# Attention and MLP on one core: the last 64 keys in one load per tensor, q and k turned by one 1024-column DMA transpose

## The chip, the core and the metric

The kernel runs on one NeuronCore of a Trainium2 chip. The metric is the device time of one execution in microseconds (us). Three executions of the kernel before took 483.74 to 487.81 us, with a median of 485.37.

## The reference

The program computes softmax attention and feeds its output to a two-layer MLP:

```python
# q, k, v: (8, 12, 448, 64)
scores = scale * np.matmul(q, k.transpose(0, 1, 3, 2))
attn = softmax(scores)                                  # over the keys
attn_out = np.matmul(attn, v)
x = attn_out.transpose(0, 2, 1, 3).reshape(B * S, H * D)  # (3584, 768)
h = x @ w_in                                            # w_in (768, 2048)
out = np.maximum(0.01 * h, h) @ w_out                   # w_out (2048, 768)
```

All inputs and the output are float32; inside, the kernel works in bf16 with float32 sums.

## The kernel before, in words

The attention is cut into 48 units, each of one batch and two heads (`NU = B * HP`, u = 6 b + hp). A sequence of 448 rows is 4 times 112 for the queries (`SC`, `NSC`) and 3 times 128 plus 64 for the keys (`NKC`, `KR`).

`load(u)` brings q, k and v of a unit from memory: q in one DMA (L108), the first 384 keys of k and of v of both heads in one DMA each (L115), and the last 64 keys, called the tail here, in one DMA per head and tensor (L120), head 0 to partitions 0 to 63 and head 1 to partitions 64 to 127. That makes seven loads. Except for unit 0 all are issued by SyncE, whose DMA queue is called SP here. `cast(u)` turns them to bf16 on POOL (L130, L131, L137 for q and k, L138 and L144 for v) and lays q and k of both heads side by side in one tile qkb: 4 x 128 columns of q in 112 partitions, then 3 x 128 columns of k, then 128 columns in which the tails of the two heads stand block by block (head 0 in partitions 0 to 63 and columns 0 to 63, head 1 in the others, zeros elsewhere).

qkb is then transposed, so that the head dimension lies on the partitions. For the first 12 units (`NPE`) TensorE does it (L207, L209) and VectorE copies the result to qkT (L212). From unit 12 on `dma_transposes` does it by two DMA transposes on SP (L194, from `turn`), the q half of 112 rows and the k half of 128 rows, 512 columns each. `scores` multiplies keys and queries (L227 for the 384 keys, L223 for the tails of both heads at once), `expo` takes the exponential on ScalarE, `pv` multiplies by v and normalises. The attention output x of a unit is transposed to xT, from unit 9 on by a DMA transpose on SP too. `mlp(i)` is a generator that works through 384 or 512 rows: 16 steps of w_in (L304), then the steps of w_out (L322), whose results `store` sends out through SP (L286), as a rule in two DMAs.

The order of each engine's work is the order in which the code issues it. The first six units run through `first`. After them the main loop mixes the MLP steps with half units: `event(g)` does in its first half the scores, the cast of unit u+3 and the load of unit u+5, and in its second half the last scores, the second half of pv of the unit before, its xT transpose, and the qkT transposes of unit u+2. `catch_up` calls the events by the share of the MLP's matmul work that is done. mlp(i+1) starts only when the events of its batches are through, and its first matmuls read the xT of the last of these units.

SP is one queue in order: loads, both kinds of transposes and stores pass through it one after the other. An instruction that waits holds all that stand behind it. The DMAs of SP and ScalarE share eight completion semaphores in turn, so each waits for the landing of the DMA eight places before it.

Of the kernel before, what the change touches and what calls it, by code (L numbers as in the profile page):

```python
# [9 lines left out]
F32 = mybir.dt.float32  # L10
# [6 lines left out]
def kernel(  # L17
# [9 lines left out]
    nc = tc.nc  # L27

    B, H, S, D = q.shape
    DM, DF = moe_w_in.shape  # L30
    P = 128
    HP = H // 2
    SC = 112
    NSC = S // SC
# [3 lines left out]
    NKC = 3  # L38
    KR = S - NKC * P
# [9 lines left out]
    ld_pool = ctx.enter_context(tc.tile_pool(name="ld", bufs=5))  # L49
# [30 lines left out]
    NC = 4  # L80
    QC = NSC * P
    qk_sb = [cast_pool.tile([P, QC + (NKC + 1) * P], BF16, name=f"qkb{i}") for i in range(NC)]

    NQ = 4
    QL = S + (NKC + 1) * P
    qkT = [qk_pool.tile([P, QL], BF16, name=f"qkT{i}") for i in range(NQ)]


# [13 lines left out]
    def load(u, queues=(nc.sync,) * 3):  # L102
        if u >= NU:
            return
        b, hp = divmod(u, HP)
        heads = slice(2 * hp, 2 * hp + 2)
        fq = ld_pool.tile([SC, 2, NSC, D], F32, name="fq")
        queues[0].dma_start(  # L108
            out=fq.rearrange("p h so d -> p h (so d)"),
            in_=q[b, heads].rearrange("h (p so) d -> p h (so d)", so=NSC),  # L110
        )
        raw[u] = [fq]
        for a, name, eng in ((k, "fk", queues[1]), (v, "fv", queues[2])):
            t = ld_pool.tile([P, (2 * NKC + 1) * D], F32, name=name)
            eng.dma_start(  # L115
                out=t[:, :2 * NKC * D].rearrange("p (h e) -> p h e", h=2),
                in_=a[b, heads, :NKC * P].rearrange("h (p c) d -> p h (c d)", c=NKC),
            )
            for h in range(2):
                eng.dma_start(  # L120
                    out=t[h * KR:(h + 1) * KR, 2 * NKC * D:], in_=a[b, 2 * hp + h, NKC * P:]
                )
            raw[u].append(t)

    def cast(u, by=(nc.gpsimd.tensor_copy,) * 2):
        if u >= NU:
            return
        fq, fk, fv = raw.pop(u)
        t, vt = qk_sb[u % NC], v_sb[u % NV]
        by[0](t[:SC, :QC].rearrange("p (so h d) -> p h so d", so=NSC, h=2), fq)  # L130
        by[1](  # L131
            t[:, QC:QC + NKC * P].rearrange("p (c h d) -> p h c d", c=NKC, h=2),
            fk[:, :2 * NKC * D].rearrange("p (h c d) -> p h c d", h=2, c=NKC),
        )
        for h in range(2):
            at, c0 = slice(h * KR, (h + 1) * KR), QC + NKC * P + h * D
            by[1](t[at, c0:c0 + D], fk[at, 2 * NKC * D:])  # L137
        nc.gpsimd.tensor_copy(  # L138
            v_whole[u % NV][:, :, :, :D],
            fv[:, :2 * NKC * D].rearrange("p (h c d) -> p h c d", h=2, c=NKC),  # L140
        )
        for h in range(2):
            at, c0 = slice(h * KR, (h + 1) * KR), VL + h * DV
            nc.gpsimd.tensor_copy(vt[at, c0:c0 + D], fv[at, 2 * NKC * D:])  # L144

    w_steps = []
    for i in range(4):
# [1 line left out]
    for i in range(4):  # L149
        at = (slice(None), ts(i % 2, MD // 2), ts(i // 2, NW))  # L150
        w_steps.append((w_out_sb[at], w_out_v[at]))

    def load_w(n=1):
        for _ in range(n):
            if w_steps:
                o, i = w_steps.pop(0)
                nc.gpsimd.dma_start(out=o, in_=i)

    load(0, (nc.sync, nc.scalar, nc.sync))
    for i in range(1, 5):  # L160
        load(i)
# [10 lines left out]
    ident = const_pool.tile([P, P], BF16)  # L172
    make_identity(nc, ident)
    for t in qk_sb:
        nc.gpsimd.memset(t[:, QC + NKC * P:], 0.0)
    for t, tw in zip(v_sb, v_whole):
        nc.gpsimd.memset(tw[:, :, :, D:], 1.0)
        nc.gpsimd.memset(t[:, VL:], 0.0)
        for h in range(2):
            nc.gpsimd.memset(t[h * KR:(h + 1) * KR, VL + h * DV + D:VL + (h + 1) * DV], 1.0)  # L180
    for t in e_sb:
        nc.gpsimd.memset(t[:, EL:], 0.0)
    cast(0, (nc.vector.tensor_copy, nc.scalar.copy))
    load_w()
    cast(1)
    cast(2)


# [4 lines left out]
    def turn(dst, src, rows):  # L193
        nc.sync.dma_start_transpose(out=dst.rearrange("p (c s) -> p c s", s=rows), in_=src)  # L194

    def dma_transposes(u):
        if NPE <= u < NU:
            turn(qkT[u % NQ][:, :S], qk_sb[u % NC][:SC, :QC], SC)
            turn(qkT[u % NQ][:, S:], qk_sb[u % NC][:, QC:], P)

    def transposes(u):
        if u >= min(NPE, NU):
            return
        tr = ps_g.tile([P, QL], BF16, name="tr", tag="g")
        t = qk_sb[u % NC]
        for so in range(NSC):
            nc.tensor.transpose(tr[:, ts(so, SC)], t[:SC, ts(so, P)], ident[:SC, :SC])  # L207
        for c in range(NKC + 1):
            nc.tensor.transpose(  # L209
                tr[:, S + c * P:S + (c + 1) * P], t[:, QC + c * P:QC + (c + 1) * P], ident  # L210
            )
        nc.vector.tensor_copy(qkT[u % NQ], tr)  # L212

    sc_t = {}
# [1 line left out]
    def scores(u, c):  # L216

        ps = ps_s.tile([P, 2, 512], F32, name="sc")
        t = qkT[u % NQ]
        sc_t[u, c] = ps  # L220
        keys = slice(S + c * P, S + (c + 1) * P)
        if c == NKC:
            nc.tensor.matmul(ps[:, 0, :S], t[:, keys], t[:, :S], start=True, stop=True)  # L223
            return
        for j in range(2):
            at = slice(j * D, (j + 1) * D)
            nc.tensor.matmul(ps[:, j, :S], t[at, keys], t[at, :S], start=True, stop=True)  # L227

    def expo(u, c):
        ps = sc_t.pop((u, c))  # L230
# [101 lines left out]
    def first(u):  # L332

        scores(u, 0)
        scores(u, 1)
        expo(u, 0)
        if u == 0:
            warm_up(4)
        expo(u, 1)
        if u >= 2:  # L340
            x_transposes(u - 2)
        if u >= 1:
            pv(u - 1, 0)
        load(u + 5)
        load_w({2: 1, 3: 2, 4: 2, 5: 2}.get(u, 0))
        scores(u, 2)
        expo(u, 2)
        if u + 1 < HP:
            transposes(u + 1)
        scores(u, 3)  # L350
        expo(u, 3)
        cast(u + 3)
        if u >= 1:
            pv(u - 1, 1)


    def event(g):
        u, r = divmod(g, 2)
        back = HP < u <= NU
        if r == 0:  # L360
            if HP < u - 1 < NPE - 3 + 1:
                x_transposes(u - 2)
            if back:
                pv(u - 1, 0)
            if u < NU:
                for c in range(NKC):
                    scores(u, c)
                expo(u, 0)
                expo(u, 1)
                late.append((u, 2))  # L370
            cast(u + 3)
            load(u + 5)
        else:
            if u < NU:
                scores(u, NKC)
                expo(u, NKC)
            if back:
                pv(u - 1, 1)
                if u - 1 >= NPE - 3:
                    x_transposes(u - 1)  # L380
            transposes(u + 1)
            dma_transposes(u + 2)

    transposes(0)
    warm_up(2)
    for u in range(HP):
        first(u)
    u = HP - 1
# [57 lines left out]
```

## Time and profile before

| what | us |
|---|---|
| median of 3 executions | 485.37 |
| lowest, highest | 483.74, 487.81 |
| the profiled execution | 488.74 |
| its span, first to last instruction | 486.9 |
| TensorE matmuls busy (PE) | 426.0 |
| ScalarE busy (ACT) | 213.9 |
| GpSimd busy (POOL) | 124.7 |
| VectorE busy (DVE) | 100.0 |

PE, ACT, POOL and DVE are the four compute engines. Instructions that issue a DMA are not counted as busy on SP; they are read from SP's timeline, where their duration is the time that the queue is held. Granted clock (PEclk) is the share of TensorE's full clock that it was given in a stretch. Times in the rows count from the span's start.

### The profile page before, as it was taken

The numbers are of one execution on the slowest core, as the hardware profiler recorded it, in microseconds if no ns is written. First come the engines' busy times: TensorE is split into PE (matmuls) and PEld (weight loads), VectorE is DVE, ScalarE is ACT, GpSimd is POOL, SyncE is SP. The second block draws the span as 40 slices with busy tenths as digits, with TensorE's granted clock in tenths as the row PEclk, the third lists the DMA queues.
The fourth block names the chain that finished last, engine by engine and source line by source line (L and its number), as shares of the span: only waits on it lengthen the run. The fifth ranks groups of instructions, "written<-read, shape, count | busy, mean of one in ns | idle before, by whom it ended". The sixth has DMA issues, their size and how long they took to land.

```text
span 486.9 us, 9127 instructions
## 1 busy us (share of the span) xinstructions
PE 426.0 (87%) x3491; PEld 245.1 (50%) x3491; DVE 100.0 (21%) x271; ACT 213.9 (44%) x324; POOL 124.7 (26%) x373
## 2 busy tenths in 40 slices
PE   7669989367999999965999989785999989999996
PEld 3445656232556565542556656452456645664463
DVE  2342233110113311220112211221012211130021
ACT  5463644032662366323663257432563445623400
POOL 6446435322213222311311232231132110000000
PEclk9797999787999999997999999998899989999999
DMA  7689997465546655456455664565645662221022
GB/s 156 174 192 192 227 228 186 124 179 132 109 116 153 163 140 131 115 148 174 117 107 123 173 156 104 136 146 142 155 109 129 133 158 59 39 81 43 0 64 67
DMA packets 120396, 64.27 MB, mean 132 GB/s; under 512 B 74272, under 2 KB 116768, under 8 KB 120352
## 3 DMA queue, kind: packets, MB, share of 16 engines
q1 hardware_dynamic: 112624, 57.17, 47.7%
q0 software_dynamic: 7296, 6.29, 8.3%
q8 instruction: 27, 0.44, 0.4%
q10 hardware_dynamic: 432, 0.23, 0.2%
q14 instruction: 17, 0.14, 0.1%
HBM read 45.61 MB, written 11.01 MB: 116 GB/s over the span
## 4 chain that ended last, share of the span: by engine, by line
PE 57%; DMA 20%; SPq 14%; issue 3%; POOL 2%; ACT 2%; DVE 1%; ACTq 0%; POOLq 0%
PE mm L304 26%; PE mm L322 21%; DMA fk<-in_k_dram 8%; SPq L120 6%; DMA fv<-in_v_dram 4%; PE pv L253 4%; PE sc L227 3%; SPq L194 3%; DMA xT<-x 3%; SPq L115 3%; DMA qkT<-qkb 3%; DMA fq<-in_q_dram 2%; SPq L286 2%; ACT e L236 1%; PE pv L246 1%
## 5 line engine op out<-in xcount | busy, mean ns | idle before, releaser
L236 ACT ACTIVATE e<-sc 128x896 bf16<-128x896 f32 x192 | 150.2, 826 | 147.7 <-PE sc L227 117.5
L304 PE MATMUL mm<-xT,w_in_sb 128*128 128x384 bf16 (+1 forms) x768 | 163.8, 369 | 20.6 <-DMA xT<-x 19.6
L322 PE MATMUL mm<-w_out_sb,h 128*128 128x384 bf16 x896 | 154.8, 329 | 0.5 <-DVE x L261 0.2
L304 PEld LDWEIGHTS <-w_in_sb 128*128 128x128 bf16 x768 | 75.1, 101 | 100.1 <-issue 41.6
L322 PEld LDWEIGHTS <-h 128*128 128x128 bf16 x896 | 86.4, 98 | 63.6 <-issue 10.4
L308 ACT ACTIVATE h<-mm 128x384 bf16<-128x384 f32 (+1 forms) x128 | 70.0, 547 | 96.6 <-PE mm L304 96.4
L138 POOL CAST v<-fv 128x384 bf16<-128x384 f32 x48 | 24.3, 506 | 163.0 <-issue 85.8
L326 DVE COPY o<-mm 128x384 f32<-128x384 f32 x56 | 31.2, 557 | 168.9 <-PE mm L322 156.2
L253 PE MATMUL pv<-v,e 128*128 128x65 bf16 x1152 | 59.2, 196 | 0.0
L253 PEld LDWEIGHTS <-e 128*128 128x128 bf16 x1152 | 52.5, 99 | 11.3 <-issue 4.5
L227 PE MATMUL sc<-qkT 64*128 64x448 bf16 x288 | 38.1, 365 | 21.1 <-DMA qkT<-qkb 19.8
L260 DVE RECIPROCAL rec<-pv 112x4 f32<-112x4 f32 x96 | 17.5, 182 | 180.9 <-PE pv L253 177.8
L130 POOL CAST qkb<-fq 112x512 bf16<-112x512 f32 x47 | 28.8, 612 | 91.0 <-DMA fq<-in_q_dram 81.6
L246 PE MATMUL pv<-v,e 128*128 128x130 bf16 x192 | 42.9, 223 | 4.9 <-POOL v L144 3.0
L261 DVE TENSOR_TENSOR x<-pv,rec 112x256 bf16<-112x256 f32 x96 | 40.7, 424 | 3.3
L227 PEld LDWEIGHTS <-qkT 64*128 64x128 bf16 x288 | 10.3, 96 | 30.5 <-DMA qkT<-qkb 21.0
L131 POOL CAST qkb<-fk 128x384 bf16<-128x384 f32 x47 | 23.8, 506 | 5.0 <-DMA fk<-in_k_dram 4.0
L144 POOL CAST v<-fv 64x64 bf16<-64x64 f32 x96 | 22.4, 233 | 8.9 <-DMA fv<-in_v_dram 6.2
L137 POOL CAST qkb<-fk 64x64 bf16<-64x64 f32 x94 | 21.8, 232 | 8.2 <-DMA fk<-in_k_dram 5.2
L246 PEld LDWEIGHTS <-e 128*128 128x128 bf16 x192 | 19.1, 100 | 9.2 <-ACT e L236 1.7
L223 PE MATMUL sc<-qkT 128*128 128x448 bf16 x48 | 17.9, 372 | 0.0
L212 DVE COPY qkT<-tr 128x960 bf16<-128x960 bf16 x12 | 7.9, 657 | 20.3 <-PE tr L209 20.3
(28 smaller groups left out, 54.6 us busy)
## 6 DMA issues: line engine op xcount, KB each, us to landing
fq<-in_q_dram SPq DMA_DIRECT2D x48, 224.0 KB, 3.4
fv<-in_v_dram SPq DMA_DIRECT2D x48, 192.0 KB, 2.7
fk<-in_k_dram SPq DMA_DIRECT2D x47, 192.0 KB, 3.0
w_in_sb<-in_moe_w_in_dram POOLq DMA_DIRECT2D x4, 768.0 KB, 9.6
w_out_sb<-in_moe_w_out_dram POOLq DMA_DIRECT2D x4, 768.0 KB, 23.5
out_dram<-o SPq DMA_DIRECT2D x8, 336.0 KB, 3.0
out_dram<-o SPq DMA_DIRECT2D x8, 288.0 KB, 2.9
out_dram<-o SPq DMA_DIRECT2D x8, 240.0 KB, 3.0
```

The source lines that it names most:

```text
L120: eng.dma_start(out=t[h * KR:(h + 1) * KR, 2 * NKC * D:], in_=a[b, 2 * hp + h, NKC * P:])
L130: by[0](t[:SC, :QC].rearrange("p (so h d) -> p h so d", so=NSC, h=2), fq)
L138: nc.gpsimd.tensor_copy(v_whole[u % NV][:, :, :, :D], fv[:, :2 * NKC * D].rearrange("p (h c d) -> p h c d", h=2, c=NKC),)
L227: nc.tensor.matmul(ps[:, j, :S], t[at, keys], t[at, :S], start=True, stop=True)
L236: nc.scalar.activation(o, i, AX.Exp, scale=scale)
L246: nc.tensor.matmul(ps[:, i].rearrange("p j d -> p (j d)"), e[:, at:at + P], vt[:, VL:], start=True, stop=False,)
L253: nc.tensor.matmul(ps[:, i, j, :], e[:, at:at + P], v_whole[u % NV][:, j, c, :], start=False, stop=(j == 1 and c == NKC - 1),)
L261: nc.vector.tensor_mul(x_t[u][:, ts(half, two)], ps[:SC, :, :, :D], rec.to_broadcast([SC, two, 2, D]))
L304: nc.tensor.matmul(ps[:, :n], w_in_sb[:, kk, ts(m, P)], xT[:, kk, at:at + n], start=(kk == 0), stop=(kk == KD - 1),)
L308: nc.scalar.activation(h[:, m, :n], ps[:, :n], AX.Prelu, alpha=0.01)
L322: nc.tensor.matmul(ps[:, :NW], h[:, m, ts(c, P)], w_out_sb[:, m, ts(w, NW)], start=(m == 0), stop=(m == MD - 1),)
L326: nc.vector.tensor_copy(o[c][:, ts(w, NW)], ps[:, :NW])
```

## The change

The two tail loads of a tensor become one, which puts both heads into partitions 0 to 63, side by side; the casts move the second head to partitions 64 to 127. The q half of qkb and qkT is widened from 4 x 112 to 4 x 128 columns, with zeros in partitions 112 to 127 of qkb's q half (a new memset per tile), so that q and k are one block of 1024 columns; one DMA transpose, or eight equal ones on TensorE, turns it. The scores read 112 of every 128 query columns.

```diff
-    QL = S + (NKC + 1) * P
+    QL = QC + (NKC + 1) * P
...
-            t = ld_pool.tile([P, (2 * NKC + 1) * D], F32, name=name)
+            t = ld_pool.tile([P, 2 * (NKC + 1) * D], F32, name=name)
...
-            for h in range(2):
-                eng.dma_start(
-                    out=t[h * KR:(h + 1) * KR, 2 * NKC * D:], in_=a[b, 2 * hp + h, NKC * P:]
-                )
+            eng.dma_start(
+                out=t[:KR, 2 * NKC * D:].rearrange("m (h d) -> m h d", h=2),
+                in_=a[b, heads, NKC * P:].rearrange("h m d -> m h d"),
+            )
...
-            by[1](t[at, c0:c0 + D], fk[at, 2 * NKC * D:])
+            by[1](t[at, c0:c0 + D], fk[:KR, (2 * NKC + h) * D:(2 * NKC + h + 1) * D])
...
-            nc.gpsimd.tensor_copy(vt[at, c0:c0 + D], fv[at, 2 * NKC * D:])
+            nc.gpsimd.tensor_copy(
+                vt[at, c0:c0 + D], fv[:KR, (2 * NKC + h) * D:(2 * NKC + h + 1) * D]
+            )
...
+        nc.gpsimd.memset(t[96:, :QC], 0.0)
...
-            turn(qkT[u % NQ][:, :S], qk_sb[u % NC][:SC, :QC], SC)
-            turn(qkT[u % NQ][:, S:], qk_sb[u % NC][:, QC:], P)
+            turn(qkT[u % NQ], qk_sb[u % NC], P)
...
-        for so in range(NSC):
-            nc.tensor.transpose(tr[:, ts(so, SC)], t[:SC, ts(so, P)], ident[:SC, :SC])
-        for c in range(NKC + 1):
-            nc.tensor.transpose(
-                tr[:, S + c * P:S + (c + 1) * P], t[:, QC + c * P:QC + (c + 1) * P], ident
-            )
+        for c in range(QL // P):
+            nc.tensor.transpose(tr[:, ts(c, P)], t[:, ts(c, P)], ident)
...
-        keys = slice(S + c * P, S + (c + 1) * P)
+        keys = slice(QC + c * P, QC + (c + 1) * P)
+        qT = t[:, :QC].rearrange("p (so s) -> p so s", s=P)[:, :, :SC]
+        o = ps[:, :, :S].rearrange("p j (so s) -> p j so s", s=SC)
...
-            nc.tensor.matmul(ps[:, j, :S], t[at, keys], t[at, :S], start=True, stop=True)
+            nc.tensor.matmul(o[:, j], t[at, keys], qT[at], start=True, stop=True)
```

How this moves SP's queue is shown at two places. The first is one round of the main loop near 220 us, between the store that goes out there and the next one; fq, fk and fv are the loaded tiles, out_dram is the result. Before:

```order
L286 DMA out_dram<-o 96x768
L286 DMA out_dram<-o 32x768
L108 DMA fq<-in_q_dram 112x2x256
L115 DMA fk<-in_k_dram 128x2x192
L120 DMA fk<-in_k_dram 64x64 x2
L115 DMA fv<-in_v_dram 128x2x192
L120 DMA fv<-in_v_dram 64x64 x2
L194 DMA_TRANSPOSE xT<-x 128x4x112
L194 DMA_TRANSPOSE qkT_113<-qkb_109 128x4x112
L194 DMA_TRANSPOSE qkT_113<-qkb_109 128x4x128
```

The same round with the change (lines are those of the changed kernel):

```order
L286 DMA out_dram<-o 96x768
L286 DMA out_dram<-o 32x768
L108 DMA fq<-in_q_dram 112x2x256
L115 DMA fk<-in_k_dram 128x2x192
L119 DMA fk<-in_k_dram 64x2x64
L115 DMA fv<-in_v_dram 128x2x192
L119 DMA fv<-in_v_dram 64x2x64
L197 DMA_TRANSPOSE xT<-x 128x4x112
L197 DMA_TRANSPOSE qkT_113<-qkb_109 128x8x128
```

The order is the same; of the twelve DMAs of the round nine are left.

The second place is the start of SP's queue, up to the first load of unit 2, the third load of q. Before:

```order
L108 DMA fq<-in_q_dram 112x2x256
L115 DMA fv<-in_v_dram 128x2x192
L120 DMA fv<-in_v_dram 64x64 x2
L108 DMA fq<-in_q_dram 112x2x256
L115 DMA fk<-in_k_dram 128x2x192
L120 DMA fk<-in_k_dram 64x64 x2
L115 DMA fv<-in_v_dram 128x2x192
L120 DMA fv<-in_v_dram 64x64 x2
L108 DMA fq<-in_q_dram 112x2x256
```

With the change:

```order
L108 DMA fq<-in_q_dram 112x2x256
L115 DMA fv<-in_v_dram 128x2x192
L119 DMA fv<-in_v_dram 64x2x64
L108 DMA fq<-in_q_dram 112x2x256
L115 DMA fk<-in_k_dram 128x2x192
L119 DMA fk<-in_k_dram 64x2x64
L115 DMA fv<-in_v_dram 128x2x192
L119 DMA fv<-in_v_dram 64x2x64
L108 DMA fq<-in_q_dram 112x2x256
```

The load of q for unit 2 was the twelfth DMA of SP and is now its ninth. (In unit 0 the loads of k are issued by ScalarE, with one instead of two for its tails.)

## Rows read from the trace of the kernel before

**Rows 1.** Waits of TensorE in seven stretches; us in total, times, longest.

```profile
PE sc L227 <- DMA qkT<-qkb: 7.6, 1, 7.6
...
PE mm L304 <- DMA xT<-x: 5.6, 1, 5.6
PE sc L227 <- DMA qkT<-qkb: 1.6, 1, 1.6
...
PE mm L304 <- DMA xT<-x: 5.7, 2, 5.0
PE sc L227 <- DMA qkT<-qkb: 5.3, 4, 2.1
...
PE mm L304 <- DMA xT<-x: 1.6, 1, 1.6
...
PE sc L227 <- DMA qkT<-qkb: 5.3, 4, 2.2
PE mm L304 <- DMA xT<-x: 4.4, 1, 4.4
...
PE mm L304 <- DMA xT<-x: 2.3, 1, 2.3
```

**Rows 2.** Windows (PEclk behind the engines), then TensorE's timeline: start, us, instructions, idle before.

```profile
96.00:108.00 12.00, 9.33 (x62) 4.46 (x63) 1.77 (x5) 4.80 (x6) 2.39 (x7) 0.76 0.65 173
120.00:150.00 30.00, 30.00 (x227) 16.07 (x226) 5.08 (x15) 16.54 (x25) 8.72 (x26) 1.00 0.50 113
...
82.19 2.77 PE L322 MATMUL mm<-w_out_sb,h 128*128 128x384 bf16 x16
97.69 4.81 PE L322 MATMUL mm<-w_out_sb,h 128*128 128x384 bf16 x16
225.63 5.71 PE L304 MATMUL mm<-xT,w_in_sb 128*128 128x512 bf16 x13 [5.01 <-DMA xT<-x]
...
119.64 3.95 PE mm L304 x18
```

**Rows 3.** SP's timeline in one unit from 188 us, and the xT at 223.

```profile
188.22 2.50 SPq L194 DMA_TRANSPOSE qkT<-qkb  x2
190.76 0.57 SPq L108 DMA_DIRECT2D fq<-in_q_dram  x1
191.39 0.45 SPq L115 DMA_DIRECT2D fk<-in_k_dram  x1
191.89 1.12 SPq L120 DMA_DIRECT2D fk<-in_k_dram  x2
193.05 0.59 SPq L115 DMA_DIRECT2D fv<-in_v_dram  x1
193.69 1.11 SPq L120 DMA_DIRECT2D fv<-in_v_dram  x2
...
223.23 1.22 SPq L194 DMA_TRANSPOSE xT<-x  x1
```

**Rows 4.** The DMA transposes by line: ns min/median/max; then us from issue to landing.

```profile
L194 SPq DMA_TRANSPOSE qkT<-qkb x72: 1183/1216/2448, 92.7 to 420.6; - x72
...
DMA to landing us min/median/max: 2.3/2.4/4.4
```

**Rows 5.** Timeline of TensorE at 16.8 and 30.1 us; groups by line (busy, mean ns).

```profile
16.83 0.56 PE L207 MATMUL tr<-ident,qkb 112*128 112x112 bf16 x4 [5.06 <-POOL qkb L130]
...
30.09 0.35 PE L253 MATMUL pv<-v,e 128*128 128x65 bf16 x6
...
L178 POOL MEMSET v<- 128x130 bf16 x5 | 1.1, 213 | 0.0
L137 POOL CAST qkb<-fk 64x64 bf16<-64x64 f32 x94 | 21.8, 232 | 8.2 <-DMA fk<-in_k_dram 5.2
```

**Rows 6.** SP's timeline at the two ends of the backlog from 77 to 113 us.

```profile
76.87 1.43 SPq L108 DMA_DIRECT2D fq<-in_q_dram  x1
...
110.57 1.22 SPq L194 DMA_TRANSPOSE xT<-x  x1
```

More of the change, by code (lines that the diff above doesn't have):

```diff
@@ L220, in scores @@
         sc_t[u, c] = ps
-        keys = slice(S + c * P, S + (c + 1) * P)
+        keys = slice(QC + c * P, QC + (c + 1) * P)
+        qT = t[:, :QC].rearrange("p (so s) -> p so s", s=P)[:, :, :SC]
+        o = ps[:, :, :S].rearrange("p j (so s) -> p j so s", s=SC)
         if c == NKC:
-            nc.tensor.matmul(ps[:, 0, :S], t[:, keys], t[:, :S], start=True, stop=True)
+            nc.tensor.matmul(o[:, 0], t[:, keys], qT, start=True, stop=True)
             return
```

## The prediction

> **What bounds the kernel now.** I read the waits of TensorE first, stretch by stretch, because its busy share says nothing about where it is late. Up to 84 us its waits are few; after that nearly all the idle time has one of two releasers: a DMA transpose of q and k (qkT) or a DMA transpose of an attention output (xT) [rows 1]. Added up from 84 us on: 7.6 + 5.6 + 1.6 + 5.7 + 5.3 + 1.6 + 5.3 + 4.4 + 2.3 = 39.4 us of a span of 486.9. The reader is to see that no row of this group names an arithmetic engine.
>
> The second view is TensorE's timeline around the long waits. The window from 96 us, after the 7.6 us wait, shows a mean granted clock of 0.76, where the window from 120 us, with no wait in it, shows 1.00 (the full 2.4 GHz level). Sixteen output matmuls that take 2.77 us before take 4.81 behind that wait: 2.0 lost. Thirteen matmuls of 512 columns behind the xT wait at 225.63 take 5.71, while 18 take 3.95 in the steady stretch, so 13 should take 2.85: 2.85 lost [rows 2]. The same 5.7 us piece stands behind the xT waits at 113 and 338.
>
> The third view is the DMA queue of SyncE (SP), which issues both transposes. From 188.22 to the xT at 223.23 it issues without a pause worth naming: two halves of qkT 2.50, q 0.57, k 0.45, the two k tails 1.12, v 0.59, two v tails of the same price, then the next xT [rows 3]. x was ready long before the xT of 223.23 was issued; the transpose stood behind the queue. So the waits of 180 to 226 us, and by the same pattern of 84 to 113 and 293 to 339, are a backlog of SP's issue time, not of bytes. Where TensorE is continuously busy (120 to 150) SP has slack and nothing is to be won.
>
> **The change part by part.** *The tails.* Per unit (one batch and two heads) four 16 KB loads become two of 32 KB. A pair costs SP 1.12 us [rows 3]. The merged load has three dimensions, as the k load beside it, which issues in 0.45 with four times as many rows; so I price it as one of the pair, 0.56. With the gap of about 0.04 that goes too, a unit saves 2 x 0.60 = 1.2 us of SP. Ends: nothing saved if it costs the pair's 1.12; 1.4 if it costs the 0.45 of k.
>
> *The transposes.* One instruction of 1024 columns replaces two of 512. The group of 72 has a minimum of 1183 ns and a median of 1216, though half of them read 112 rows and half 128: rows do not set the price [rows 4]. Whether columns do, no row shows, as all have 512. Low end: one price for any width, 1.22, saves 1.27 with its gap. High end: twice, 2.44, saves nothing. I split the 1.22: a plain load's 0.57 [rows 3] as the fixed part, the other 0.65 growing with the columns; then 0.57 + 2 x 0.65 = 1.87, saving 0.63 per unit. The DMA lands 2.4 us after its issue begins [rows 4]; the wide one should land 1.2 us after its issue ends, so no later than the second half does today.
>
> By the Trainium skill, "DMA: Bandwidth & Descriptors", section "Why a DMA increments its semaphore by 16 and not by 1" (the comparison with earlier generations), the sequencer of the generations before pushes one command per tile for a transpose inside SBUF, 262,144 cycles for 8,192 tiles. That speaks against this half of the change: by it the price goes with the tiles and 2.44 is nearer than 1.22. The equal price of 112 and 128 rows neither shows nor excludes it. What it gives is the second case below.
>
> *What SP's saving is worth, stretch by stretch,* each unit in a backlog saving 1.2 + 0.63 = 1.83:
> - 77 to 113 us: from the q load at 76.87 to the xT at 110.57 [rows 6] SP issues five loads and two qkT: 5 x 1.2 + 2 x 0.63 = 7.3. Before 77 the queue is held by landings, as eight DMAs are in flight at most (each waits for the eighth before it); eight now cover 1.6 units instead of 1.1. At the start TensorE idles 5.06 us for the cast of unit 2 [rows 5]; unit 2's first load is the twelfth DMA of SP now and the ninth then, and the last wait for a landing ahead of it is for an earlier one. I put 2.5 on both together (0 to 5). Sum 9.8, below the 14.8 of waits and 2.0 of clock there, so it counts in full.
> - 188 to 226 us: four loads and four qkT, 7.3 of the 10.3 of waits; about half of the clock's 2.85, since a wait of some 3 us is left. Sum 8.8.
> - 263 to 284: two units, more than the wait of 1.6. Sum 1.6.
> - 293 to 339: five of each, 9.15 of 9.7; what is left is too short to cost the clock, 2.85 more. Sum 12.0.
> - 386 to 397: one unit, 1.8 of 2.3. And about 0.7 of the 5.7 of 170 to 230 lies at 170, in front of the backlog; it goes too.
>
> Total 9.8 + 8.8 + 1.6 + 12.0 + 1.8 + 0.7 = 34.7.
>
> *What it adds.* Four memsets of 32x512 on POOL ahead of the first casts: from 213 ns for 130 columns, at most 840 each, likelier 0.5: 2 us of POOL in the first 6 us. The first weight load and the cast of unit 1 move by that much; behind them stand the later casts. The first lands beside earlier loads, and I have charged it inside the 2.5 above. Half of the tail casts now read partitions 0 to 63 and write 64 to 127; no row shows a shifted cast. Nothing to 232 ns more each [rows 5], POOL is idle most of the time, I take nothing. The evacuation of the first 12 units grows from 960 to 1024 columns, under 0.1 us each, beside TensorE's matmuls of the unit before; without that cover it is 1 us in all. The one transpose waits for the k tail's cast where its q half had only the cast of q to wait for; in the stretches of backlog both casts are done units earlier, so nothing; elsewhere what stands behind it on SP is the next unit's loads, which are needed two units later. The scores read q with a step (112 of each 128 columns). Ends: nothing, or each of the four pieces at the price of a matmul of its own, as six of 65 columns take 0.35 us [rows 5], 58 ns each; I take nothing, because a piece inside an instruction has no issue of its own.
>
> What is late next: in 188 to 226, TensorE itself with short rests of xT; at 113, still xT, by some 5 us.
>
> Against the profiled execution, 488.7 with what lies around its span: 488.7 - 34.7 = 454.0. That execution lies 3.4 above the median of 485.4, and some of its surplus is in these waits; I forecast 453.
>
> **The rivals.**
> 1. *The wide transpose costs 2.44* (the page's rule worked out from rows). Only the tails save: 8.5 + 4 x 1.2 + 1.6 + 5 x 1.2 + 1.2 + 0.7 = 22.8, no clock back; 466. For it: nothing in the rows excludes a price by columns. Against it: a plain load shows that a good part of an issue is fixed.
> 2. *It costs 1.22.* 11.0 + 12.7 + 1.6 + 12.6 + 2.3 + 0.7 = 41; 448. For it: rows did not matter.
> 3. *The change doesn't do what it says:* the merged tail costs the pair's 1.12 and the transpose 2.44. SP issues as long as before; within 1%, 485. Against it: k and its tail differ fourfold in rows at about one price.
> 4. *Stepped reading of q slows the scores.* 336 matmuls at half the upper end of about 0.1 us: some 17 us lost where TensorE is the bound; 470.
> 5. *Slower: the wide transpose costs more than the sum of two.* If its price grew as the square of the width, 4.9 us, each unit would cost SP 4.9 - 2.5 - 1.2 = 1.2 more; over the 17 units of the five stretches that is 20 us: 509. It decides from a price of 2.5 + 1.2 = 3.7 us on. For it: the width is unseen in the trace. Against it: 112 and 128 rows are priced alike, which no growing cost suggests.
>
> **How the numbers follow.** Chances: forecast 0.50, rival 1 0.20, rival 2 0.15, rival 3 0.05, rival 4 0.05, rival 5 0.05. The range runs from 441 (rival 2 with the start worth 5 and the median's 3.4 less) to 471 (rivals 1 and 4); outside lie rivals 3 and 5 and the edges. About 1% is what a measurement of this kernel can tell from no change. Faster: the forecast and rivals 1, 2 and 4, 0.90; same 0.05; slower 0.05.
>
> **What would show it.** 96 merged tails on SP near 0.56 us; 36 qkT transposes near 1.9 (1.2 or 2.4 for rivals 2 and 1, over 3.7 for rival 5). TensorE's waits for qkT after 100 us gone, the one at 88 to 96 us under 3; xT waits under 3 but for the one near 105 us; granted clock 1.00 in the stretch that holds the fourth and sixth batch's start. A score matmul group that takes longer than before speaks for rival 4. The forecast is wrong if these waits go and the time does not, or if they stay with a shorter SP queue, which would mean that bytes and not issues hold the transposes.

## The result, and the profile after

The changed kernel takes 440.03 us in the median (439.93 to 441.43, four executions), the kernel before 485.34 (483.74 to 487.81, four). The ratio is 0.9069, with a 95% interval of 0.9027 to 0.9112: 45 us faster, just outside the range of the prediction (441 to 471) on the fast side. The profiled execution took 441.43, its span 439.7 against 486.9. Ratios leave out three executions that took over 1.5% longer than the fastest of the same kernel (494.68 us in run 4, 599.83 in run 6, and 832.88 of the kernel before, beside runs 1 to 4).

The waits of TensorE, after [rows 1]. The first fence is the stretch of 50 to 100 us, with the smaller rows left out; the second is the whole list of 100 to 170. In 170 to 230 and 290 to 340 the list is empty, and the two other stretches hold the same single row of 0.3 as 100 to 170.

```profile
PE mm L304 <- DMA xT<-x: 4.2, 1, 4.2
PE sc L227 <- DMA qkT<-qkb: 2.5, 1, 2.5
```

```profile
PE mm L304 <- ACT h L308: 0.3, 1, 0.3
```

Of the 39.4 us that TensorE waited for the two kinds of DMA transposes, 6.7 are left, all of them before 100 us.

Windows of the changed kernel (busy us of PE, PEld, DVE, ACT and POOL, then the granted clock) answer to [rows 2]:

```profile
84.00:96.00 12.00, 8.30 (x62) 4.14 (x63) 2.18 (x6) 4.80 (x6) 3.36 (x9) 0.86 0.83 223
96.00:108.00 12.00, 9.12 (x43) 3.90 (x43) 0.61 (x2) 4.05 (x7) 2.90 (x10) 0.72 0.51 120
...
120.00:240.00 120.00, 119.52 (x1017) 70.33 (x1015) 27.25 (x76) 63.05 (x96) 34.49 (x101) 1.00 0.64 153
240.00:360.00 120.00, 119.67 (x1030) 71.18 (x1028) 27.19 (x76) 63.09 (x96) 33.56 (x99) 1.00 0.67 157
```

From 120 to 360 us TensorE is busy 239.2 of 240 us at the full clock (1.00); from 84 us to there the slow clock stands only behind the two waits that are left.

SP's timeline of one unit, after, answers to [rows 3]: xT, qkT, the five loads, and the next xT.

```profile
173.92 1.23 SPq L197 DMA_TRANSPOSE xT<-x  x1
175.26 1.23 SPq L197 DMA_TRANSPOSE qkT<-qkb  x1
176.54 0.57 SPq L108 DMA_DIRECT2D fq<-in_q_dram  x1
177.17 0.46 SPq L115 DMA_DIRECT2D fk<-in_k_dram  x1
177.68 0.63 SPq L119 DMA_DIRECT2D fk<-in_k_dram  x1
178.35 0.59 SPq L115 DMA_DIRECT2D fv<-in_v_dram  x1
178.98 0.61 SPq L119 DMA_DIRECT2D fv<-in_v_dram  x1
180.47 1.23 SPq L197 DMA_TRANSPOSE xT<-x  x1
```

The last load ends at 179.59 and the next xT starts at 180.47: SP rests 0.9 us, where before it went from one DMA to the next. The longest row of the list of SP's waits in 170 to 230 says for what:

```profile
SPq L197 <- DVE x L261: 9.9, 5, 2.8
```

SP now waits for the attention output x, that is for TensorE and VectorE, and no longer the other way round. (A second row puts 5.2 us down to POOL's casts, but the timeline shows no such rests: in the unit above, qkT follows xT within 0.11 us.)

The prices, by line (ns min/median/max), answer to [rows 4]; the last row is the time to landing of both kinds of transposes:

```profile
L197 SPq DMA_TRANSPOSE xT<-x x39: 1185/1227/2082, 79.7 to 390.9; - x39
L197 SPq DMA_TRANSPOSE qkT<-qkb x36: 1231/1236/1930, 81.3 to 371.7; - x36
...
DMA to landing us min/median/max: 2.3/3.0/4.9
...
L119 SPq DMA_DIRECT2D fv<-in_v_dram x48: 607/607/1489, 1.7 to 346.1; - x48
L119 SPq DMA_DIRECT2D fk<-in_k_dram x47: 607/628/2081, 3.6 to 344.8; - x47
```

The transpose of 1024 columns costs SP 1236 ns, 20 more than one of 512. The merged tail costs 607 to 628 ns (medians).

What was added [rows 5]: the memsets, the tail casts of k, of which half now shift their partitions, and the stepped scores (min/median/max).

```profile
L178 POOL MEMSET qkb<- 32x512 bf16 x4 | 2.1, 520 | 0.2
...
L137 POOL CAST qkb<-fk 64x64 bf16<-64x64 f32 x94 | 21.8, 232 | 4.3 <-DMA fk<-in_k_dram 1.5
...
L227 PE MATMUL sc<-qkT x288: 349/349/577, 7.7 to 379.8; 64*128 64x448 bf16 x144
```

The casts cost 232 ns as before, and the score matmuls have a median of 349 ns.

Where the 47.2 us of the two spans went, by the start of the first matmul of each MLP (L304 on TensorE's timeline):

| start of mlp | 0 | 1 | 2 | 3 | 4 | 5 | 6 | 7 | end |
|---|---|---|---|---|---|---|---|---|---|
| before | 42.03 | 106.26 | 168.97 | 219.37 | 281.45 | 332.82 | 394.26 | 440.50 | 486.9 |
| after | 36.62 | 93.44 | 154.21 | 198.17 | 252.63 | 296.58 | 350.74 | 392.96 | 439.7 |
| lead | 5.4 | 12.8 | 14.8 | 21.2 | 28.8 | 36.2 | 43.5 | 47.5 | 47.2 |

### The profile page after: what moved, and what is told of

Its sections match the earlier page's. It is cut to its first block, busy times and chain, and to the rows that moved or that the text cites. A ratio compares the mean times of both kernels' runs of the same rounds, so it can differ in the third digit from the quotient of the medians.

```text
span 439.7 us, 8832 instructions
## 1 busy us (share of the span) xinstructions
PE 413.6 (94%) x3491; PEld 241.4 (55%) x3491; DVE 100.5 (23%) x271; ACT 213.3 (49%) x324; POOL 127.5 (29%) x377
## 4 chain that ended last, share of the span: by engine, by line
PE 77%; DMA 10%; SPq 5%; ACT 3%; issue 2%; POOL 1%; DVE 1%; ACTq 0%; POOLq 0%
PE mm L322 32%; PE mm L304 30%; DMA fk<-in_k_dram 7%; PE pv L253 6%; PE sc L227 5%; ACT e L236 2%; DMA fv<-in_v_dram 2%; PE pv L246 2%; DMA xT<-x 2%; PE sc L223 1%; SPq L119 1%; ACT h L308 1%; SPq L115 1%; SPq L286 1%; SPq L197 1%
## 5 line engine op out<-in xcount | busy, mean ns | idle before, releaser
L304 PE MATMUL mm<-xT,w_in_sb 128*128 128x384 bf16 (+1 forms) x768 | 155.2, 356 | 5.3 <-DMA xT<-x 4.2
L304 PEld LDWEIGHTS <-w_in_sb 128*128 128x128 bf16 x768 | 73.3, 98 | 79.4 <-issue 17.0
L253 PEld LDWEIGHTS <-e 128*128 128x128 bf16 x1152 | 51.7, 98 | 8.8 <-issue 1.6
L246 PEld LDWEIGHTS <-e 128*128 128x128 bf16 x192 | 18.9, 98 | 8.6 <-ACT e L236 1.4
L223 PE MATMUL sc<-qkT 128*128 128x448 bf16 x48 | 16.9, 353 | 0.0
L209 PE MATMUL tr<-ident,qkb 128*128 128x128 bf16 x96 | 9.1, 227 | 6.9 <-POOL qkb L131 2.7
## 6 DMA issues: line engine op xcount, KB each, us to landing
w_out_sb<-in_moe_w_out_dram POOLq DMA_DIRECT2D x4, 768.0 KB, 21.2
```

Source lines behind the costliest of these rows:

```text
L246: nc.tensor.matmul(ps[:, i].rearrange("p j d -> p (j d)"), e[:, at:at + P], vt[:, VL:], start=True, stop=False,)
L253: nc.tensor.matmul(ps[:, i, j, :], e[:, at:at + P], v_whole[u % NV][:, j, c, :], start=False, stop=(j == 1 and c == NKC - 1),)
L304: nc.tensor.matmul(ps[:, :n], w_in_sb[:, kk, ts(m, P)], xT[:, kk, at:at + n], start=(kk == 0), stop=(kk == KD - 1),)
```

## The experiments

Two theories stand. **S**: SP's issue time was the bound, and the change pays by the microseconds of issue that it takes from SP's rounds. **D**: the number or shape of the DMAs was (fewer and larger ones, or the full 128 rows, land sooner). The first four runs take the change apart and move the suspected cost to another engine; the next four price the transpose by width, settle where the lead at the start comes from, and repeat the move on an idle engine; the last four go at the waits that are left. Each run stands against the kernel before as it was timed beside it, with a median of 484.47 us for runs 1 to 4, 485.21 for 5 to 8 and 485.26 for 9 to 12.

**1. The tails alone.** The kernel before with the two merged tail loads (and the shifted casts that go with them), nothing else:

```diff
-            for h in range(2):
-                eng.dma_start(
-                    out=t[h * KR:(h + 1) * KR, 2 * NKC * D:], in_=a[b, 2 * hp + h, NKC * P:]
-                )
+            eng.dma_start(
+                out=t[:KR, 2 * NKC * D:].rearrange("m (h d) -> m h d", h=2),
+                in_=a[b, heads, NKC * P:].rearrange("h m d -> m h d"),
+            )
```

> Only the tail loads are merged; q and k are turned by two transposes as before. Theory S (SP's issue time is what fell): SP saves 1.1 us per unit (two issues of 1.12 a pair, against 0.61 each). That takes about 5 us off the start, 5 x 1.1 before 113 us, 4.4 of the 10.3 us of waits of 188 to 226, 1.6 at 284, 5.5 of 9.7 at 293 to 339 and 1.1 at 397, no clock back: 485 - 23 = 462. Waits for qkT and xT after 180 us remain at about half. Theory D (the number of DMAs counts, since eight may be in flight, and not their issue time): two of the three DMAs saved per unit are these, so about two thirds of the 45 us: 455.

Measured: 454.59 us (454.0 to 455.74), ratio 0.9376 (0.9329 to 0.9423). That is the figure of D, and better than S had it. The profile says why it does not decide. TensorE's waits for transposes, one row for each of the windows from 50, 100, 170, 290 and 340 us (up to 440):

```profile
PE sc L229 <- DMA qkT<-qkb: 4.8, 2, 3.2
...
PE mm L306 <- DMA xT<-x: 5.4, 1, 5.4
...
PE mm L306 <- DMA xT<-x: 3.8, 1, 3.8
...
PE mm L306 <- DMA xT<-x: 3.0, 1, 3.0
...
PE mm L306 <- DMA xT<-x: 1.3, 1, 1.3
```

The qkT waits of 170 to 230 and 290 to 340 are gone altogether, where S, as I had summed it, left half. A round of SP, from one xT to the next, now takes 7.0 us where it holds no store:

```profile
163.58 1.22 SPq L196 DMA_TRANSPOSE xT<-x  x1
...
170.59 1.22 SPq L196 DMA_TRANSPOSE xT<-x  x1
```

TensorE's round, from one unit's scores to the next, was 7.4 in the kernel before near 200 us. Its score groups stand 8.0 and 9.2 apart there, and of these 0.7 and 1.9 were waits for qkT:

```profile
191.98 0.74 PE L227 MATMUL sc<-qkT 64*128 64x448 bf16 x6 [0.66 <-DMA qkT<-qkb]
...
200.02 0.74 PE L227 MATMUL sc<-qkT 64*128 64x448 bf16 x6 [0.68 <-DMA qkT<-qkb]
...
209.26 0.74 PE L227 MATMUL sc<-qkT 64*128 64x448 bf16 x6 [1.88 <-DMA qkT<-qkb]
```

A round of 7.0 is below that, so by S no backlog should build up there until stores come in. TensorE's round is not the same everywhere: in the changed kernel, between 165 and 223 us, where SP mostly waits for x, the xT transposes start 6.6 to 9.9 us apart.

**2. The transpose alone.** The changed kernel with its tails loaded in pairs as before:

```diff
-            eng.dma_start(
-                out=t[:KR, 2 * NKC * D:].rearrange("m (h d) -> m h d", h=2),
-                in_=a[b, heads, NKC * P:].rearrange("h m d -> m h d"),
-            )
+            for h in range(2):
+                eng.dma_start(
+                    out=t[h * KR:(h + 1) * KR, 2 * NKC * D:], in_=a[b, 2 * hp + h, NKC * P:]
+                )
```

> Only the transpose of q and k is merged (the wide layout and its memsets included); tails are loaded in pairs as before. Theory S: SP saves 1.28 us per unit from unit 12 on and nothing before: 2.5 up to 113 us, 5.1 of 10.3, 1.6, 6.4 of 9.7, 1.3: 485 - 17 = 468; mlp(0) starts at about 42 us as before, plus up to 2 us for the memsets. Theory D: one of three DMAs, and only from unit 12 on: 10 to 15 us, 472.

Measured: 455.27 us (454.57 to 459.75), ratio 0.9412 (0.933 to 0.9493). Neither theory's figure: S had 468, D 472. mlp(0) starts at 39.2 us, earlier than the 42 that was expected, with the new memsets in it. Each half alone takes 29 to 30 us, together they take 45 and not 59: what is left of waits after the first half is too little for the second. That fits a threshold (SP's round against TensorE's), and the sums of S, which took units times microseconds, were too small for either half. It does not exclude D, since under any theory the waits can run out.

**3. Two transposes in the wide layout.** The changed kernel, 1024 columns turned in two halves of 128 rows:

```diff
-            turn(qkT[u % NQ], qk_sb[u % NC], P)
+            turn(qkT[u % NQ][:, :QC], qk_sb[u % NC][:, :QC], P)
+            turn(qkT[u % NQ][:, QC:], qk_sb[u % NC][:, QC:], P)
```

> The changed kernel with its 1024 columns turned by two transposes of 512 (all 128 rows). If the price of an instruction does not depend on its width, each costs 1.22 and SP has 1.28 us more per unit than in the changed kernel: waits of some 6 and 4 us come back at the two long backlogs with their clock, 460. If the wide one's low price came from the full 128 rows or the aligned layout, two of them cost about 0.62 each and the time stays at 440.

Measured: 454.77 us (452.15 to 456.08), ratio 0.937 (0.9312 to 0.9428), the same as the tails alone and 5 us below the 460 of S. The layout shows no gain in the time; each half costs as before:

```profile
L197 SPq DMA_TRANSPOSE qkT<-qkb x72: 1193/1216/2666, 79.0 to 383.8; - x72
```

**4. The tails issued by ScalarE.** The kernel before, one word changed:

```diff
-                eng.dma_start(
+                (nc.scalar if u >= 12 else eng).dma_start(
```

> The kernel before, with the four tail loads of each unit from 12 on issued by ScalarE's queue: the same DMAs, bytes, tiles and eight semaphores, and SP has 2.3 us less to issue per unit. Theory S: the waits after 100 us go almost wholly, 10 us up to 113 us, 10 at 188 to 226, 12 with the clock at 293 to 339, 4 elsewhere: 485 - 36 = 449, or some us more, since ScalarE now issues for 2.3 us per unit and waits for landings in its own queue. Theory D: the number of DMAs in flight is unchanged, so 485.

Measured: 489.9 us (486.91 to 494.68), ratio 1.0102 (1.007 to 1.0134): 1% longer, where S had 449 or some us more and D 485. The profiled execution is the longest of the ten, 494.68, so its waits are larger than those of the median. From 100 us on TensorE's list of waits now begins:

```profile
PE mm L304 <- ACT h L308: 15.3, 15, 3.3
PE mm L304 <- DMA xT<-x: 4.6, 3, 2.8
PE pv L246 <- ACT h L308: 3.1, 5, 1.6
```

and in 60 to 100 us:

```profile
PE pv L246 <- ACT h L308: 24.6, 5, 20.6
```

There is no wait for qkT left, and the xT waits fell from 19.6 to 4.6 in three. So SP was relieved as S says, and ScalarE paid: its activations stand behind issues that wait for landings. ScalarE's own list has one such rest of 20.8 us, ended by the landing of a k load, and TensorE's 20.6 us follow from it; the last weight loads, issued up to 49.8 us, were landing then, 16 to 25 us after their issue. The run shows both effects and not the worth of the first.

**5. The tails merged in the first 12 units only.** The kernel before; the condition stands in the load and in both tail casts:

```diff
+            if u < 12:
+                eng.dma_start(
+                    out=t[:KR, 2 * NKC * D:].rearrange("m (h d) -> m h d", h=2),
+                    in_=a[b, heads, NKC * P:].rearrange("h m d -> m h d"),
+                )
+            else:
...
```

> The kernel before with the tails merged for units 0 to 11 only; from unit 12 on pairs of tails and two transposes as before. If the changed kernel's lead at the start comes from the merged tails of the first units, mlp(0) starts at about 36 us instead of 42 and the lead of 5 us is kept, since the backlog of 77 to 113 us then starts earlier by as much: 480; the waits after 113 us are those of the kernel before. If the start is bound by bytes, or the lead is eaten by the backlog, 485.

Measured: 480.3 us (477.44 to 481.81), ratio 0.9891 (0.9832 to 0.9951). mlp(0) starts at 35.1 us, and 4.9 us of the lead reach the end (2.4 to 8.2 by the interval); the waits after 113 us are nearly those of before (xT 6.1 and qkT 5.0 us in 170 to 230). All runs together confirm where the lead comes from: in the five profiles with pairs of tails in the first 12 units mlp(0) starts at 39.2 to 42.0 us, in the nine with merged tails at 34.0 to 36.6, with the new memsets or without. It is some 5 us, twice what I had put on it. Whether there SP's issues or the eight DMAs in flight make it was not taken apart; it stays open. Up to 77 us SP waits for landings in both kernels (22.5 us before, 29.3 after, by its lists of waits).

**6. Four transposes of 256 columns.**

```diff
-            turn(qkT[u % NQ], qk_sb[u % NC], P)
+            for i in range(4):
+                turn(qkT[u % NQ][:, ts(i, QL // 4)], qk_sb[u % NC][:, ts(i, QL // 4)], P)
```

> The changed kernel with its 1024 columns turned by four transposes of 256. One price for every width (1.22 to 1.24): four cost 4.9 on SP, 3.8 us per unit more than in the changed kernel and 1.3 more than in the kernel before; with the merged tails saving 1.1, SP stands slightly worse than before from unit 12 on, but the early lead stays: about 485. A fixed part of 0.57 and the rest by columns (my split in the prediction): 256 columns cost 0.9 each, 3.6 for four, 2.4 more than in the changed kernel: about 467.

Measured: 517.58 us (513.75 to 599.83), ratio 1.064 (1.0558 to 1.0723). The price is that of the first case, its time is not:

```profile
L197 SPq DMA_TRANSPOSE qkT<-qkb x144: 1167/1196/2263, 79.6 to 448.0; - x144
```

With 1196, 1216 and 1236 ns for 256, 512 and 1024 columns, twice the width costs 20 ns. I had counted the added issue only in the stretches that had waits before. SP's timeline shows rounds longer than TensorE's anywhere, here with a store:

```profile
206.84 1.23 SPq L197 DMA_TRANSPOSE xT<-x  x1
208.18 5.03 SPq L197 DMA_TRANSPOSE qkT<-qkb  x4
213.30 1.00 SPq L287 DMA_DIRECT2D out_dram<-o  x2
...
217.41 1.23 SPq L197 DMA_TRANSPOSE xT<-x  x1
```

The round is 10.6 us, and stretches in which TensorE had been the bound wait too (6 waits for qkT in 340 to 440 us, where the kernel before had none). This fits the threshold from its other side, but here too the number of DMAs grows with the issue time.

**7. The tails issued by POOL.** As run 4, with the idle engine:

```diff
-                eng.dma_start(
+                (nc.gpsimd if u >= 12 else eng).dma_start(
```

> The kernel before with the four tail loads of each unit from 12 on issued by POOL, which is idle most of the time: same bytes and tiles, SP has 2.3 us less per unit, no issue lands on ScalarE. Theory S (SP's issue time): the qkT waits after 100 us go and the xT waits shrink under 2; 485 - 33 = 452. POOL pays some 0.9 us per issue, 3.5 per unit, beside 2.5 of casts in a unit of 7.4. Theory D (fewer DMAs, larger ones): 485.

Measured: 444.92 us (444.71 to 445.97), ratio 0.9174 (0.9129 to 0.9218). The same loads, the same bytes, the same two narrow transposes, none merged, and 40 of the 45 us, 7 more than S had summed. TensorE's waits for qkT after 100 us are gone; of those for xT 4.6, 1.4 and 0.3 us are left, where under 2 was expected. An issue costs POOL 0.52 us and not 0.9:

```profile
L120 POOL DMA_DIRECT2D fk<-in_k_dram x72: 517/522/551, 68.4 to 341.9; - x72
```

This decides for S in the main loop, for the tails: the queue on which these DMAs stand matters, and not their number or shape. One rival is left to look at, since in the traces POOL's DMAs count on eight semaphores of their own, so that they do not take places among the eight in flight of SP and ScalarE. But SP's list of waits in the kernel before, from 77 to 440 us, names a landing only once:

```profile
SPq L194 <- DMA fk<-in_k_dram: 0.6, 1, 0.6
```

So the eight places are no bound there. No run moves the transposes of q and k to another queue; for them S rests on SP's timeline, and on the runs 3, 6 and 9 to 11.

**8. The first weight load later.** The kernel before:

```diff
-    load_w()
     cast(1)
     cast(2)
+    load_w()
```

> The kernel before with the first weight load issued after the casts of units 1 and 2 instead of before them. If the 5 us wait at 16.8 us comes from the weight load landing in front of unit 2's loads, it goes: 481, unless mlp(0) then waits for its weights. If it comes from SP's late issue of unit 2's loads, it stays at 4 to 5 us: 485.

Measured: 482.88 us (481.29 to 485.08), ratio 0.9954 (0.9923 to 0.9985). The wait for the casts of q remains, 4.4 us in two, the longest 3.7; mlp(0) starts at 39.4 us. In runs 4 and 7, whose start is that of the kernel before, it starts at 40.7 and 40.0, so the starts scatter by 2 us and the shift is hardly more. The weight load is not the main cause of the wait.

**9 to 12. What is left at 86 to 99 us.** All four are the changed kernel. Three move units from the DMA transposes to TensorE, the qkT and the xT of one, two and four more:

```diff
-    NPE = 12
+    NPE = 13        # 14 and 16 in the next two
```

> The changed kernel with NPE = 13: unit 12 is turned by TensorE, and xT goes by DMA from unit 10 on instead of 9. SP loses one qkT and one xT (2.6 us) in the only backlog left, 72 to 99 us; the qkT wait of 2.5 us at 86 shrinks under 1.5 and the xT wait of 4.2 us at 99 by some 2.6; TensorE and VectorE pay about 1 us for the twelve small transposes. Theory S: 440 - 4 = 436. If the waits there come from the landings of the weights and loads and not from SP's queue: 441.

> The same with NPE = 14: SP loses two qkT and two xT (5.2 us) before 99 us. Theory S: both waits go (6.7 us), most of the slow clock behind them too (about 3), TensorE pays 2: 440 - 7 = 433. If landings hold the stretch: 442.

> The same with NPE = 16: beyond what SP needs. Nothing more to win by S and four units' transposes on TensorE, some 4 us, in a stretch where it is then the bound: 435. If SP still had a backlog at 14: below the run with 14.

The fourth lets POOL issue some of the merged tails:

```diff
-            eng.dma_start(
+            (nc.gpsimd if 12 <= u < 18 else eng).dma_start(
                 out=t[:KR, 2 * NKC * D:].rearrange("m (h d) -> m h d", h=2),
```

> The changed kernel with the merged tails of units 12 to 17 issued by POOL: SP has 1.3 us less per unit in the stretch of 65 to 99 us, five units, nothing added on TensorE. Theory S: the two waits of 2.5 and 4.2 us go for the most part and with them some clock: 440 - 7 = 433. If landings hold the stretch: 440.

Measured: 437.05 us with NPE = 13 (436.47 to 438.11), 432.93 with 14 (432.29 to 433.85), 435.32 with 16 (434.06 to 436.27), and 436.54 with POOL (432.79 to 436.94). The three steps of NPE come out as S has them (436, 433, 435), to about 1 us. TensorE's waits for the transposes in 50 to 100 us, of the run with 13 and of that with 14:

```profile
PE mm L304 <- DMA xT<-x: 4.6, 1, 4.6
PE sc L227 <- DMA qkT<-qkb: 0.6, 1, 0.6
```

```profile
PE mm L304 <- DMA xT<-x: 0.3, 1, 0.3
```

With 14 the backlog is gone, and the window in which the changed kernel's clock was 0.72 is at full clock:

```profile
96.00:108.00 12.00, 12.00 (x94) 6.12 (x91) 1.21 (x4) 7.32 (x12) 3.99 (x12) 1.00 0.54 119
```

With 16 nothing is left to win and TensorE does more. With POOL the qkT wait fell to 1.1 us in two, but the xT wait stayed, at 5.0; half of what S had expected came. The trace shows that this wait is mostly a landing. The x is ready at 87.45; its transpose starts after a store, and the two xT of 78 to 96 us take over 5 us to land, where the median of the kernel before was 2.4:

```profile
87.92 0.88 SPq L286 DMA_DIRECT2D out_dram<-o  x2
88.89 1.37 SPq L197 DMA_TRANSPOSE xT<-x  x1
...
DMA to landing us min/median/max: 5.3/5.4/5.6
...
94.25 2.29 PE L304 MATMUL mm<-xT,w_in_sb 128*128 128x512 bf16 x5 [5.03 <-DMA xT<-x]
```

Why they land late there stays open. The kernel with NPE = 14 beats both: 0.8914 of the kernel before (0.8877 to 0.8951), and 7 us less than the changed one.

## Why the prediction was wrong, point by point

**The bound was read rightly.** The reading that the waits of TensorE are SP's issue time, and not bytes, is shown for the tails by run 7, where the same DMAs from an idle engine gave 40 us. Runs 3 and 6 agree with it for the transposes, with the same bytes in two and four issues, but there the number of DMAs grows with the issue time.

**The step that failed is the price of the wide transpose,** "I split the 1.22: a plain load's 0.57 as the fixed part, the other 0.65 growing with the columns; then 0.57 + 2 x 0.65 = 1.87". It measured 1.236. Almost nothing grew with the columns: 20 ns from 256 to 512 and from 512 to 1024. The unit saves 2.50 + 0.04 - 1.24 = 1.30 on the transpose and not 0.63. With that price the prediction's own sums are those of its rival 2, 41 us and not 34.7. With 2.9 more at the start and 1.7 of clock at 397, both below, they come to 45.6 of the 47.2 measured. The rule of the Trainium skill that I weighed there ("DMA: Bandwidth & Descriptors", section "Why a DMA increments its semaphore by 16 and not by 1", one command per tile) would, as I read it for this chip, have the price go with the tiles. The traces do not agree: four times the columns, from 256 to 1024, cost 40 ns more. That the 112 and 128 rows cost the same was the better hint; I had it in hand and set it aside.

**The start was undersized.** I put 2.5 us on it "(0 to 5)"; mlp(0) starts 5.4 us earlier, and run 5 shows 4.9 us (2.4 to 8.2) at the end from the first 12 units' tails alone. The memsets cost the 520 ns each that I had estimated; runs 1 and 3, without and with them, start mlp(0) at 35.1 and 34.0, so they do not show in the time.

**The clock was given back more fully.** Behind the wait of 5.0 us at 225 I counted half of 2.85; all of it came back, and so did the slow clock behind the 2.3 us at 397, which I had not counted. By stretches:

| stretch (before) | forecast | measured | how |
|---|---|---|---|
| up to 113 | 9.8 | 14.3 | matmul behind the xT wait: 113.16, after 98.88 |
| 170 to 226 | 8.8 + 0.7 | 13.9 | waits of 11.0 and clock of 2.85 gone |
| 263 to 284 | 1.6 | 1.6 | the wait is gone |
| 293 to 339 | 12.0 | 12.6 | waits of 9.7 and clock of 2.85 gone |
| 386 to 397 | 1.8 | 3.7 to 4.0 | mlp(6) is 4.0 shorter by the table of starts, 2.3 of it the wait |

These add to 46.1 to 46.4 of 47.2; the rest is in pieces too small to name.

**The sum as such was right only in part.** It took the saving of a stretch as units times microseconds. Runs 1 and 2 show that this undersizes either half of the change (30 and 29 us, where the sums of S were 23 and 17). By the rounds read in run 1, SP's saving counts until its round is shorter than TensorE's, and from there on there is no backlog to shorten. For the whole change, at 1.24, both ways of counting end with nearly no waits after 113 us.

**The rest of the list.** The tails cost 0.61 to 0.63 and not 0.56. Gone after 100 us are the qkT waits, as forecast; the first is 2.5 (under 3 was forecast), and the xT wait that stays is 4.2 ("by some 5"). The wide transpose lands 3.1 us after its issue begins (median of 170 to 230 us), no later than the second half before, as forecast. The granted clock is 1.00 from 120 to 360 us. Of the rivals, 1, 3 and 5 are out by the measured prices and 4 by the 349 ns per score matmul; rival 2 is what happened, and I had given it 0.15. The range ended at 441, rival 2 with a start of 5 and the execution's 3.4 above the median taken off (its own sum gives 441.8); the 1.7 us of clock at 397 are what was missing.

## What to carry to other kernels

When many waits name a DMA, look at the timeline of the queue that issues it before looking at bytes: if it goes from issue to issue without a rest, count its issues per round, and compare that round with the round of the engine that waits. Here saving paid until SP's round was no longer the longer one. Moving the tail issues from unit 12 on to an idle engine (40 us) paid more than merging all tails in pairs (30 us), and moving them to a busy one paid nothing, because that engine's own work then stood behind landings. A DMA transpose on this queue was paid per instruction and hardly by width, so it should be as wide as the layout allows, padding included.

## What was not expected of the hardware

A DMA transpose of 256, 512 and 1024 columns of 128 rows took 1196, 1216 and 1236 ns to issue. A load of 64 rows of two runs took 607 to 628 ns against 1.12 us for the two loads that it replaces, and the same plain loads took 522 ns each on POOL. A matmul that reads its moving operand in four stepped pieces of 112 columns took 349 ns, against 350 in one piece (the row of the kernel before):

```profile
L227 PE MATMUL sc<-qkT x288: 348/350/578, 7.2 to 427.4; 64*128 64x448 bf16 x144
```
